# A fused attention and gated feed-forward kernel: VectorE's and ScalarE's side work placed in front of each value block, two kinds of work handed to GpSimd

## The chip, the cores and the metric

The kernel runs on one core of a Trainium2 chip. A core has five engines with an instruction queue each: TensorE (PE, matrix multiplication; PEld are its weight loads), VectorE (DVE), ScalarE (ACT), GpSimd (POOL) and SyncE (SP, which here only issues the DMA transfers). The metric is the device time of one execution in microseconds (us), as the median of several runs. Before the change it is 1805.28 us, the median of three runs from 1804.98 to 1807.15.

## The reference

A token sequence of 2048 rows of 512 is normalized, goes through 32-head softmax attention and, in parallel, through a bilinear gated feed-forward of width 1792, and both are joined:

```python
def _A_ref(x, wqkv, wo):                       # H = 32 heads of Dh = 16
    q, k, v = split(x @ wqkv)
    scores = einsum("bhqd,bhkd->bhqk", q, k) * Dh ** -0.5
    o = einsum("bhqk,bhkd->bhqd", softmax(scores), v)
    return o.transpose(0, 2, 1, 3).reshape(B, S, D) @ wo

def _B_ref(x, w_gate, w_up, w_down):
    h = (x @ w_gate) * (x @ w_up)              # no nonlinearity
    return h @ w_down

xn = layernorm(x)
return x + _A_ref(xn, ...) * silu(_B_ref(xn, ...))
```

Everything is float32. For the projections and the feed-forward the kernel splits each operand into a high part, rounded to a shorter format (F32R), and the low rest, and adds three products: high by high, high by low, low by high.

## The kernel before

**Units, rounds and cycles.** The attention is cut into units: a unit `i` is a group of four heads (`g`, 8 groups) and a block of 512 queries (`c`, 4 blocks), so `NU` = 32 units. A unit has 16 rounds, one for each block of 128 keys; `n` counts all 512 rounds of the main loop (L844 onwards). In a round, for each of the four heads `j`, TensorE makes one transposed score tile of 128 keys by 512 queries (`expo`, L605), of which ScalarE takes the exponential (L607), and one score tile of a later unit (`score`, L580; it runs `LEAD` = 21 rounds ahead), of which VectorE takes the row maximum (L582). Score tiles rotate through three banks (`s`), transposed score tiles and the value blocks' results through three more (`st`), and the fillers below through two (`misc`).

**Value blocks.** After every even round `values()` issues a value block (`block`, L618): TensorE multiplies the exponentials of two earlier rounds (the list `prev`: the two rounds ahead of the current one) with the values and adds them up in a bank. During this block TensorE makes no scores. The block's result is added to the unit's running sum `sums[i]`, a tile named `acc` with one buffer. For a unit's first block ScalarE copies the result into it (L622). For its last block VectorE adds the result (L624). For the six between, ScalarE copies the result out into a tile `e` of the exponentials' ring (L627, `EBUFS` = 12 buffers) and GpSimd adds it (the line of GpSimd's instructions is always L64, that of a helper).

**Finishing a unit.** `finish(i)` is a generator which `step_small(heads)` advances by one `yield` after every round and once in `values()`: VectorE transposes the sum (L636), takes the reciprocals of the softmax denominators (L639), GpSimd multiplies (tile `on`; for the last four units VectorE does, L641), and five rounds later (one round, for the last four units) VectorE transposes back (L645) and a DMA stores the result.

**Fillers.** Between the score tiles TensorE works on a generator of other matrix products: first the remaining query and key projections (`proj_pair`), then the feed-forward (`ffn`: gate `g` and up `u` together, then down `y`), at last the output projection (`ending`, tiles `z`). The class `Filler` spreads each pair of products over whole cycles of two rounds, from an odd round's second head to the next even round's third head. The numbers of filler products in a cycle differ therefore: a gate and up pair takes two or three cycles. When a pair is done, its results have to leave the two `misc` banks: ScalarE copies `g` (L375), VectorE multiplies `h = u * g` (L377), ScalarE rounds `h` to `hh` (L335) and GpSimd takes the rest `hl`; down products are added to `y` (L402; L398 and L400 for the first). GpSimd splits all weights too: `w1h`, `w1l`, `w0h`, `w0l` for gate and up, `dh` and `dl` for down, `fh` and `fl` for the output weights. `silu` goes over the finished `y` in four steps, each a tanh on ScalarE (L341) and two steps on GpSimd.

**What sets the order.** TensorE, ScalarE and VectorE execute in the order of the program text (`manual_schedule`). GpSimd's and SyncE's instructions are ordered by a scheduler. `soon(k, fn)` puts work off by `k` steps, a step being one head of a round (`step()`), so that `fn`'s instructions come behind that head's score tile in each queue. Before the change the product `h` is issued one step after its pair has ended, its rounding four steps after, the second of two additions one step after the first, and a step of `silu` two steps after the third round of four. `flush()` issues everything that still waits.

Of the kernel before, what the change touches and what calls it, by code (L numbers as in the profile page):

```python
# [19 lines left out]
P = 128  # L20
# [29 lines left out]
def body(ctx, tc, x, wqkv, wo, wg, wu, wd, out):  # L50
# [80 lines left out]
    def flush():  # L131
        while waiting:
            waiting.pop(0)[1]()

    def step():
        steps[0] += 1
        while waiting and waiting[0][0] <= steps[0]:
            waiting.pop(0)[1]()


    ep = ctx.enter_context(tc.tile_pool(name="ep", bufs=1))

# [157 lines left out]
    def proj_pair(m, which):  # L300

        outs = []
        yield from pair(outs, [("misc", f"p{w}_{m}_{c}") for _, w, c in which],
                        [terms(lambda d: ws[0][:, d], lambda d: ws[1][:, d],
                               lambda d: xh[c][:, d], lambda d: xl[c][:, d], ND) for ws, _, c in which])
        raws = [qp.tile([P, D], F32, name="qr", bufs=QBUFS) for _ in outs]
        fst["high"] = nc.scalar.activation(raws[0], outs[0], AF.Copy)
        nc.vector.tensor_copy(raws[1], outs[1])
        for o, (_, w, c) in zip(raws, which):
            hl = qp.tile([P, 2, D], F32R, name="hl", bufs=HBUFS)  # L310
            split_rows(o, hl[:, 0], hl[:, 1])
            qk_store(hl, m, w, c)

    def qk_store(hl, m, which, c):

# [15 lines left out]

    later = []

    def hidden(h, hi, lo):
        nc.scalar.activation(hi, h, AF.Copy)  # L335
        pool.tensor_tensor(lo, h, hi, op=OP.subtract)

    def silu(fp, c, y):
        for t in range(4):
# [12 lines left out]
    def ffn(nxt):  # L352
        fp = fst["fp"]
        for c in range(NC):
# [7 lines left out]
            for ti, fs in enumerate(THIRDS):  # L362
# [4 lines left out]
                for i, f in enumerate(fs):  # L367
                    ws = nxt
                    if not (c == NC - 1 and f == NF - 1):
                        nxt = gu_weights((f + 1) % NF)  # L370
                    outs = []
                    yield from pair(outs, [("misc", f"{n}{c}_{f}") for n in "gu"], [terms(lambda d: wh[:, d], lambda d: wl[:, d],
                                                 lambda d: fh[:, d], lambda d: fl[:, d], ND) for wh, wl in ws])
                    g = fp.tile([P, 512], F32, name="g", bufs=1)
                    nc.scalar.activation(g, outs[0], AF.Copy)  # L375
                    h = fp.tile([P, 512], F32, name="h", bufs=1)
                    soon(1, lambda h=h, u=outs[1], g=g: nc.vector.tensor_tensor(h, u, g, op=OP.mult))  # L377
                    soon(4, lambda h=h, hi=hh[:, i], lo=hl[:, i]: hidden(h, hi, lo))
                    raw = fp.tile([P, D], F32, name="wdr", bufs=2)
                    dma(raw, wd[f * P:(f + 1) * P])  # L380
                    pool.tensor_copy(dh[:, i], raw)
                    pool.tensor_tensor(dl[:, i], raw, dh[:, i], op=OP.subtract)
# [7 lines left out]
                for t in range(0, 4, 2):  # L390
                    outs = []
                    yield from pair(outs, [("misc", f"y{c}_{ti}_{u}") for u in (t, t + 1)], [terms(lambda i: hh[:, i, u * P:(u + 1) * P],
                                                 lambda i: hl[:, i, u * P:(u + 1) * P],
                                                 lambda i: dh[:, i], lambda i: dl[:, i], len(fs)) for u in (t, t + 1)])
                    for n, o in enumerate(outs):
                        def add(o=o, y=y[:, t + n], first=ti == 0, n=n):
                            if first and n:
                                nc.vector.tensor_copy(y, o)  # L398
                            elif first:
                                nc.scalar.activation(y, o, AF.Copy)  # L400
                            else:
                                nc.vector.tensor_tensor(y, o, y, op=OP.add)  # L402
                        soon(n if ti else 0, add)
            later.append(silu(fp, c, y))


# [203 lines left out]
    def block(todo):  # L610
# [9 lines left out]
        if todo[0][1] == 0:  # L620
            sums[i] = keep.tile([P, 512], F32, name="acc", bufs=1)
            nc.scalar.activation(sums[i], o, AF.Copy)  # L622
        elif kt >= NT - 2:
            nc.vector.tensor_tensor(sums[i], o, sums[i], op=OP.add)  # L624
        else:
            part = etile()
# [3 lines left out]
    def finish(i):  # L630
# [3 lines left out]
        tn = tr.rearrange("p b e -> p (b e)")  # L634
        yield
        nc.vector.transpose(tn, sums.pop(i))  # L636
        yield
        rc = keep.tile([P, 16, 1], F32, name="rc", bufs=1)
        nc.vector.reciprocal(rc, tr[:, :, DH:DH + 1])  # L639
        late = i >= NU - NC  # L640
        (nc.vector if late else pool).tensor_tensor(on[:, :, 0:DH], tr[:, :, 0:DH], rc.to_broadcast([P, 16, DH]),  # L641
                                                         op=OP.mult)
        for _ in range(1 if late else 5):
            yield
        nc.vector.transpose(tn, on.rearrange("p b e -> p (b e)"))  # L645
        if i == NU - 1:
            fst["tn"] = tn
# [114 lines left out]
    def filler(wq0):  # L762
        yield from proj_pair(0, [(wq0, 0, 2), (wq0, 0, 3)])
        for m in range(1, NG // 2):
            wk, wq = fst.get(("qk", m)) or (qk_weights(m, 1), qk_weights(m, 0))
            for c in range(NC):
# [5 lines left out]
                        tc.add_manual_dep(put.ins, after, BEHIND, reason="not before the first exponentials")  # L772
                if m == NG // 2 - 1 and c == NC - 2:
                    nxt = gu_weights(0)
        flush()
        qkv.close()
        fst["fp"] = ffp.enter_context(tc.tile_pool(name="ffn", bufs=1, reuse_waits="tile"))
# [53 lines left out]
    prev = []  # L831

    def values():
        block(prev)
        if prev[-1][1] == NT - 1:
            heads.append(finish(prev[0][0]))
# [3 lines left out]
    with tc.manual_schedule(engines=ORDERED):  # L840
# [3 lines left out]
        for n in range(NU * 16):  # L844
# [20 lines left out]
                    fil.part(n % 2 and j == 1)  # L865
            if sr == 15 and si < NU:
                maxima(si, 8 if si < NU - 1 else 4)
            step_small(heads)
            if kt % 4 == 2:
                soon(2, lambda: step_small(later))  # L870
            if n == 0:
                run(fst["v"])
            elif n % 2 == 0 or n == NU * 16 - 1:
                values()
            prev.append((i, kt, es))
        block(prev)
        run(finish(NU - 1))
        flush()
# [23 lines left out]
```

## Time and profile before

| | us |
|---|---|
| median of three runs | 1805.28 |
| the profiled execution's own time | 1807.26 |
| its span, from the first to the last instruction | 1805.0 |
| busy: TensorE | 1767.9 |
| busy: VectorE | 1455.0 |
| busy: ScalarE | 1323.7 |
| busy: GpSimd | 821.8 |

The granted TensorE clock was 0.993 of full speed over the span. The times below come from one execution taken by the hardware profiler. A group's row names the line of the kernel, the engine, the operation, the tiles out<-in, their shapes and the count, then the busy time and the mean duration in ns, and at last the idle time of the engine just ahead of the group and what ended it. Where a tile or line is asked for by itself, a row gives shortest, median and longest duration in ns. In an order of time a row begins with its start and its duration in us, and merges consecutive instructions of one kind; brackets hold the idle time ahead and what ended it. A row of the busy time by stretch gives the stretch, its length, and for TensorE, weight loads, VectorE, ScalarE and GpSimd the busy time with the number of instructions, then the granted clock, the transfers' share and GB/s. A matmul's end is modelled, so a busy TensorE is not one at its peak.

### The profile page before, as it was taken

Reading aid. Unit: us, or ns where it says so; the run is one execution under the profiler, and the core shown is the slowest. Engines: PE = TensorE matmul, PEld = TensorE weight load, DVE = VectorE, ACT = ScalarE, POOL = GpSimd, SP = SyncE. Lnnn points to the kernel's source line nnn. Section 1 sums busy time; section 2 is a strip of 40 time slices with the busy share of each in tenths; the row PEclk is TensorE's granted clock in tenths of the full one; section 3 lists DMA queues with packets and bytes.
Section 4 is the critical chain, followed back from the end, with each engine's and each line's share of the span. In section 5 each row is a group of like instructions: output and inputs, shape, how many; then the busy total and the mean of one; then the engine's idle time right before and its main releaser. Section 6 shows DMA issues by size and latency. Waiting matters only on the chain.

```text
span 1805.0 us, 35056 instructions
## 1 busy us (share of the span) xinstructions
PE 1767.9 (98%) x13578; PEld 1056.4 (59%) x13578; DVE 1455.0 (81%) x2471; ACT 1323.7 (73%) x2601; POOL 821.8 (46%) x833
## 2 busy tenths in 40 slices
PE   9999999899999999999999999999999999999997
PEld 6666556556565555555555565665555555555544
DVE  6778888788888888888888888888888888888823
ACT  6357777677777777777777787777778777777673
POOL 5314444643534546344343653534545354345641
PEclk9999999999999999999999999999999999999999
DMA  5316523511231222311024220411224111111431
GB/s 198 115 57 205 217 103 124 145 40 34 69 75 51 75 65 69 75 51 51 28 73 102 80 63 23 103 40 51 85 55 103 40 51 51 35 56 49 143 110 70
DMA packets 117234, 145.78 MB, mean 81 GB/s; under 512 B 12620, under 2 KB 74060, under 8 KB 114380
## 3 DMA queue, kind: packets, MB, share of 16 engines
q1 hardware_dynamic: 117068, 143.55, 27.6%
q8 instruction: 106, 1.74, 0.4%
q14 instruction: 60, 0.49, 0.1%
HBM read 95.94 MB, written 47.45 MB: 79 GB/s over the span
## 4 chain that ended last, share of the span: by engine, by line
PE 86%; DVE 4%; POOL 3%; ACT 2%; DMA 2%; issue 1%; SPq 0%; POOLq 0%; DVEq 0%; ACTq 0%
PE pv L618 25%; PE t L605 17%; PE s L580 12%; PE g L270 5%; PE u L270 4%; PE y L270 4%; PE y L274 4%; PE u L274 3%; PE g L274 3%; DVE mx L582 3%; PE p L270 3%; PE v L251 2%; PE z L270 1%; ACT e L607 1%; PE p L274 1%
## 5 line engine op out<-in xcount | busy, mean ns | idle before, releaser
L582 DVE TENSOR_REDUCE mx<-s 128x1 f32<-128x512 f32 x2048 | 1276.8, 681 | 247.3 <-PE s L580 163.2
L607 ACT ACTIVATE e<-t 128x512 f32<-128x512 f32 x2048 | 1110.8, 609 | 126.4 <-PE t L605 32.2
L605 PE MATMUL t<-qs,ks 50*128 50x512 f32 x2048 | 805.8, 415 | 15.8 <-ACT e L607 14.3
L580 PE MATMUL s<-ks,qs 48*128 48x512 f32 x2048 | 805.0, 423 | 6.1 <-DVE mx L582 5.8
L605 PEld LDWEIGHTS t<-qs,ks 50*128 50x128 f32 x2048 | 360.0, 185 | 327.6 <-issue 162.6
L618 PE MATMUL pv<-e,V 128*32 128x512 f32 x4096 | 495.4, 601 | 0.0
L64 POOL TENSOR_TENSOR acc<-acc,e 128x512 f32<-128x512 f32 x192 | 251.0, 1307 | 455.8 <-ACT e L627 455.8
L580 PEld LDWEIGHTS s<-ks,qs 48*128 48x128 f32 x2048 | 350.7, 185 | 51.9 <-DVE mx L582 23.4
L627 ACT ACTIVATE e<-pv 128x512 f32<-128x512 f32 x192 | 114.7, 598 | 221.6 <-PE pv L618 221.6
L618 PEld LDWEIGHTS pv<-e,V 128*32 128x32 f32 x4096 | 107.4, 109 | 237.0 <-issue 182.7
L64 POOL CAST w0h<-w0r 128x512 fp32r<-128x512 f32 x60 | 36.7, 611 | 154.9 <-PE g L274 68.8
L274 PE MATMUL g<-fh,w1h 64*128 64x512 f32 x224 | 90.7, 405 | 0.0
L274 PE MATMUL y<-dh,hh 64*128 64x512 f32 x224 | 89.7, 401 | 0.0
L270 PE MATMUL y<-dh,hl 64*128 64x512 f32 x224 | 87.9, 392 | 1.7 <-POOL hl L64 1.7
L270 PE MATMUL u<-fh,w0h 64*128 64x512 f32 x224 | 89.1, 398 | 0.0
L274 PE MATMUL u<-fh,w0h 64*128 64x512 f32 x224 | 88.8, 396 | 0.0
L274 PE MATMUL u<-fh,w0l 64*128 64x512 f32 x224 | 88.5, 395 | 0.0
L270 PE MATMUL g<-fh,w1l 64*128 64x512 f32 x224 | 88.4, 395 | 0.0
L270 PE MATMUL g<-fl,w1h 64*128 64x512 f32 x224 | 88.3, 394 | 0.0
L270 PE MATMUL g<-fh,w1h 64*128 64x512 f32 x224 | 88.2, 394 | 0.0
L270 PE MATMUL y<-dh,hh 64*128 64x512 f32 x224 | 88.2, 394 | 0.0
L274 PE MATMUL u<-fl,w0h 64*128 64x512 f32 x224 | 88.1, 393 | 0.0
(257 smaller groups left out, 3065.7 us busy)
## 6 DMA issues: line engine op xcount, KB each, us to landing
w1r<-in_wg_dram SPq DMA_DIRECT2D x56, 256.0 KB
w0r<-in_wu_dram SPq DMA_DIRECT2D x56, 256.0 KB
wdr<-in_wd_dram SPq DMA_DIRECT2D x56, 256.0 KB
qs<-QD SPq DMA_DIRECT2D x64, 192.0 KB
ks<-KD SPq DMA_DIRECT2D x12, 768.0 KB
KD<-hl SPq DMA_DIRECT2D x16, 512.0 KB
QD<-hl SPq DMA_DIRECT2D x16, 512.0 KB
OD<-tr SPq DMA_DIRECT2D x31, 256.0 KB
```

Of the source, the lines that this page charges most:

```text
L64: got = getattr(self.engine, name)(*args, **kw)
L251: nc.tensor.matmul(o, l(d), r(d), start=k == d == 0, stop=k == 2 and d == ND - 1)
L270: nc.tensor.matmul(outs[k], l[LOWER], r[LOWER], start=k == 0 and n == 0, stop=(stop or k == 0) and n == len(low) - 1, skip_group_check=k == 1)
L274: nc.tensor.matmul(outs[1 - k], l[UPPER], r[UPPER], start=k == 0 and m == 0, stop=(stop or k == 0) and m == len(high) - 1, skip_group_chec ...
L580: nc.tensor.matmul(o, QS[i][b:b + KB, pr, t * P:(t + 1) * P], k[b:b + KB, pr, kc * 512:(kc + 1) * 512], start=True, stop=True)
L582: nc.vector.tensor_reduce(MX[i][:, j, t, kc:kc + 1], o, axis=AX.X, op=OP.max)
L605: nc.tensor.matmul(o, k[b:b + KR, pr, kt * P:(kt + 1) * P], QS[i][b:b + KR, pr], start=True, stop=True)
L607: nc.scalar.activation(e, o, AF.Exp, scale=DH ** -0.5)
L618: nc.tensor.matmul(o[32 * j:32 * j + 32], V[:, kt, h0:h0 + 32], es[j], start=n == 0, stop=n == len(todo) - 1)
L627: nc.scalar.activation(part, o, AF.Copy)
```

## The change

A list `before_values` collects work, and `run_ahead()` issues all of it. `values()` calls `run_ahead()` and then advances `finish` by one step, both directly in front of the value block; `step_small(heads)` after every round is gone, so a unit's finish goes on once a cycle, besides the one step when it is put on the list. `finish` has fewer `yield`s: the first transposition and the reciprocal stand together in front of one block, the second transposition in front of the next. On the list go: the product `h` and its rounding; the additions to `y`, both together; of a projection pair, the copy of the second result by VectorE with the splitting and storing behind it. A step of `silu` follows the round at once, which is in front of a block too. TensorE's order of instructions stays as it is.

Two things change engines. `hidden`, which rounded `h` on ScalarE, is replaced by `product`, which multiplies on VectorE and leaves the rounding and the rest to GpSimd (`split_rows`). And the last block's addition to the running sum is done on VectorE only for the last two blocks of the last unit; for the other 31 units ScalarE copies it out and GpSimd adds it, as for the blocks between.

```diff
+    before_values = []
+
+    def run_ahead():
+        while before_values:
+            before_values.pop(0)()
...
         fst["high"] = nc.scalar.activation(raws[0], outs[0], AF.Copy)
-        nc.vector.tensor_copy(raws[1], outs[1])
-        for o, (_, w, c) in zip(raws, which):
-            hl = qp.tile([P, 2, D], F32R, name="hl", bufs=HBUFS)
-            split_rows(o, hl[:, 0], hl[:, 1])
-            qk_store(hl, m, w, c)
+
+        def rest():
+            nc.vector.tensor_copy(raws[1], outs[1])
+            for o, (_, w, c) in zip(raws, which):
+                hl = qp.tile([P, 2, D], F32R, name="hl", bufs=HBUFS)
+                split_rows(o, hl[:, 0], hl[:, 1])
+                qk_store(hl, m, w, c)
+        before_values.append(rest)
...
-    def hidden(h, hi, lo):
-        nc.scalar.activation(hi, h, AF.Copy)
-        pool.tensor_tensor(lo, h, hi, op=OP.subtract)
+    def product(h, u, g, hi, lo):
+        nc.vector.tensor_tensor(h, u, g, op=OP.mult)
+        split_rows(h, hi, lo)
...
-                    soon(1, lambda h=h, u=outs[1], g=g: nc.vector.tensor_tensor(h, u, g, op=OP.mult))
-                    soon(4, lambda h=h, hi=hh[:, i], lo=hl[:, i]: hidden(h, hi, lo))
+                    before_values.append(lambda h=h, u=outs[1], g=g, hi=hh[:, i], lo=hl[:, i]: product(h, u, g, hi, lo))
...
-                        soon(n if ti else 0, add)
+                        before_values.append(add)
...
-        elif kt >= NT - 2:
+        elif i == NU - 1 and kt >= NT - 2:
             nc.vector.tensor_tensor(sums[i], o, sums[i], op=OP.add)
...
         nc.vector.transpose(tn, sums.pop(i))
-        yield
         rc = keep.tile([P, 16, 1], F32, name="rc", bufs=1)
...
-        for _ in range(1 if late else 5):
-            yield
+        yield
         nc.vector.transpose(tn, on.rearrange("p b e -> p (b e)"))
...
+        run_ahead()
         flush()
         qkv.close()
...
     def values():
+        run_ahead()
+        step_small(heads)
         block(prev)
...
-            step_small(heads)
             if kt % 4 == 2:
-                soon(2, lambda: step_small(later))
+                step_small(later)
...
+        run_ahead()
         block(prev)
         run(finish(NU - 1))
         flush()
```

## The prediction

> **What bounds the kernel now.** I read the page first, then the busy time by stretch, then VectorE's instructions in order of time.
>
> ```profile
> span 1805.0 us, 35056 instructions
> PE 1767.9 (98%) x13578; PEld 1056.4 (59%) x13578; DVE 1455.0 (81%) x2471; ACT 1323.7 (73%) x2601; POOL 821.8 (46%) x833
> PE 86%; DVE 4%; POOL 3%; ACT 2%; DMA 2%; issue 1%; SPq 0%; POOLq 0%; DVEq 0%; ACTq 0%
> ```
>
> TensorE looks full, but its busy time can't be taken at its word. I call a cycle the two rounds from the start of one value block (L618) to the next; there are 256. These are six cycles and one with a tanh, cut from block start to block start:
>
> ```profile
> 807.85:814.43 6.58, 6.34 (x53) 3.71 (x56) 5.17 (x10) 5.25 (x11) 2.75 (x4) 1.00 0.05 16
> 840.17:846.98 6.81, 6.58 (x54) 3.77 (x53) 5.82 (x10) 4.99 (x11) 1.45 (x3) 1.00 0.02 3
> 664.44:671.17 6.73, 6.36 (x51) 3.12 (x51) 5.76 (x11) 5.37 (x12) 5.75 (x7) 1.00 0.34 86
> 1094.35:1100.32 5.97, 5.97 (x48) 3.30 (x52) 4.81 (x9) 4.74 (x11) 1.30 (x1) 1.00 0.20 62
> 1100.32:1107.14 6.82, 6.82 (x61) 4.35 (x64) 6.67 (x13) 4.98 (x10) 0.00 (x0) 1.00 0.03 7
> 1177.85:1183.83 5.98, 5.98 (x53) 3.72 (x52) 4.88 (x9) 4.40 (x10) 2.09 (x3) 1.00 0.09 34
> 1183.83:1190.54 6.71, 6.71 (x61) 4.19 (x60) 6.45 (x13) 5.72 (x13) 5.60 (x6) 1.00 0.27 78
> ```
>
> The first number is the length, the second TensorE's busy time with its instructions in brackets. Full cycles (61 matmuls) take 6.71 us, light ones (48 to 53) only 5.98, and 48 matmuls seem to fill TensorE as well as 61. So light cycles are not bound by TensorE. VectorE's order of time says by what:
>
> ```profile
> 810.21 2.48 DVE L582 TENSOR_REDUCE mx<-s 128x1 f32<-128x512 f32 x4 [1.41 <-PE t L605]
> 812.61 0.70 DVE L645 STREAM_TRANSPOSE tr<-on 128x512 f32<-128x512 f32 x1
> ...
> 836.34 4.87 DVE L582 TENSOR_REDUCE mx<-s 128x1 f32<-128x512 f32 x8 [1.21 <-PE s L580]
> 842.20 0.69 DVE L624 TENSOR_TENSOR acc<-pv,acc 128x512 f32<-128x512 f32 x1 [0.99 <-PE pv L618]
> ...
> 845.20 0.70 DVE L636 STREAM_TRANSPOSE tr<-acc 128x512 f32<-128x512 f32 x1
> 845.83 2.44 DVE L582 TENSOR_REDUCE mx<-s 128x1 f32<-128x512 f32 x4
> 848.19 0.67 DVE L377 TENSOR_TENSOR h<-u,g 128x512 f32<-128x512 f32 x1
> 848.79 0.23 DVE L639 RECIPROCAL rc<-tr 128x16 f32<-128x16 f32 x1
> 849.37 5.15 DVE L582 TENSOR_REDUCE mx<-s 128x1 f32<-128x512 f32 x8 [0.35 <-PE s L580]
> ```
>
> Eight maxima cost 4.87. Between two runs of eight VectorE idles 1.2 to 1.4 us, while TensorE is in the value block and makes no scores. In a light cycle scores wait for maxima: 4.87 plus the hole is the 5.98. The hole can be filled: the block of 846.98 meets the product at 848.19, 1.21 later; product and reciprocal go into the hole and the next maximum starts at 849.37, 2.39 after the block's start. So **2.39 - 1.21 = 1.18 us of VectorE work right ahead of a block costs nothing**. Work in the middle of a run does cost: the second transposition (812.61) makes a light cycle 6.58 instead of 5.98; the last sum (842.20) with the first transposition (845.20) makes one 6.81. In a full cycle that pair costs 6.82 - 6.71, mostly hidden behind TensorE.
>
> **The gains.** Prices of the parts:
>
> ```profile
> L624 DVE TENSOR_TENSOR acc<-pv,acc 128x512 f32<-128x512 f32 x33 | 22.8, 691 | 30.3 <-PE pv L618 28.7 <-POOL w0l L64 0.8
> L335 ACT ACTIVATE hh<-h 128x512 fp32r<-128x512 f32 x56 | 36.4, 651 | 0.0
> L341 ACT ACTIVATE e<-y 128x512 f32<-128x512 f32 x16 | 10.3, 645 | 0.0
> L64 POOL CAST dh<-wdr 128x512 fp32r<-128x512 f32 x56 | 33.6, 612 | 62.1 <-PE y L274 32.0 <-DMA wdr<-in_wd_dram 22.6 <-PE y L270 7.1
> L64 POOL TENSOR_TENSOR acc<-acc,e x192: 1253/1307/1337, 125.1 to 1779.6; 128x512 f32<-128x512 f32 x192
> L636 DVE STREAM_TRANSPOSE tr<-acc x32: 698/699/712, 162.4 to 1783.7; 128x512 f32<-128x512 f32 x32
> L645 DVE STREAM_TRANSPOSE tr<-on x32: 698/700/712, 181.7 to 1785.2; 128x512 f32<-128x512 f32 x32
> ```
>
> (a) Last sums leave VectorE for all units but the last, and the first transposition moves ahead of the next block with the reciprocal: 0.70 + 0.23 = 0.93, under 1.18, so free. The eighth cycle of a unit becomes an ordinary one. Of 30 such cycles before the tail, 14 are light (0.60 to 0.84 over an ordinary one, 0.73 on average: 10.2 us), 2 between (0.34), 14 full (0.09 each): **12.1 us**. (b) The second transposition goes ahead of the block after that, 0.70, free: 18 light third cycles lose 0.37 to 0.61: **9.0 us**; the full ones gain nothing. (c) The tanh stands in mid-run now and delays exponentials: 664.44:671.17 is a light cycle of 6.73 where such a cycle without it takes 6.21 by the trace's other block starts. Ahead of a block ScalarE has a hole too (1.23 us in the ACT rows below). Six light cycles: **2.8 us**. (d) The rounding of h leaves ScalarE (0.65 each, 56 times), nearly always hidden now: **0.5 us**. Together 24.4. The product h stands behind the same maximum as before: nothing. The additions to y move by one maximum: nothing.
>
> **The costs on VectorE.** The unit's running sum has one buffer, so ScalarE's first copy of the next unit can't start before the first transposition has read the old one. It starts 1.96 after the block (row 666.40); the transposition ends 1.21 + 0.70 = 1.91. That fits by 0.05. Where a product or a projection's copy stands ahead of it (9 units in the new order), it ends 0.6 later, the copy too, and with it the score bank that TensorE wants back: 0.55 each, **5.0**. Two units have two additions to y ahead: 1.2 late, 0.2 of it lost already, **1.8**. Two light cycles with additions and the maxima's reduction overrun the hole by 0.3: **0.6**.
>
> **The costs on GpSimd.** It gets 31 sums of 1.307 and 56 castings of 0.612, 74.8 us more. What matters is when a running sum is done: the part it reads lies in the exponentials' ring, and the eighth exponential behind it takes the buffer over. What lateness does is here already:
>
> ```profile
> 666.40 0.60 ACT L627 ACTIVATE e<-pv 128x512 f32<-128x512 f32 x1 [1.23 <-PE pv L618]
> 667.85 0.65 ACT L341 ACTIVATE e<-y 128x512 f32<-128x512 f32 x1
> ...
> 256.60 0.60 ACT L607 ACTIVATE e<-t 128x512 f32<-128x512 f32 x1 [1.89 <-POOL acc L64]
> 257.09 0.59 ACT L627 ACTIVATE e<-pv 128x512 f32<-128x512 f32 x1
> ```
>
> ```profile
> ACT e L607 <- POOL acc L64: 22.4, 9, 6.8
> ```
>
> Nine exponentials wait so, 22.4 us in all. An eighth exponential has about 1.2 us to spare, since ScalarE waits for the block anyhow; beyond this the part's copy is late and the cycle longer. A cycle with a product, on GpSimd, with its block at 827.90:
>
> ```profile
> 827.49 0.61 POOL L64 CAST w0h<-w0r 128x512 fp32r<-128x512 f32 x1 [2.36 <-PE u L270]
> 829.85 1.31 POOL L64 TENSOR_TENSOR w1l<-w1r,w1h 128x512 fp32r<-128x512 f32 x1
> 831.10 1.32 POOL L64 TENSOR_TENSOR acc<-acc,e 128x512 f32<-128x512 f32 x1
> 832.47 1.28 POOL L64 TENSOR_TENSOR hl<-h,hh 128x512 fp32r<-128x512 f32 x1
> ```
>
> In the new order casting and rest of h stand ahead of that sum: it starts at 831.1 + 0.6 + 1.3 = 833.0 and ends at 834.3, 6.4 after the block. Even in a light cycle 7.5 would do: its length 6.0, the eighth exponential 0.3 after the next block's start, 1.2 to spare. So the castings cost nothing in an ordinary cycle. Where a chain of down weights and a tanh's two steps come ahead too, it is late:
>
> ```profile
> 1347.03 1.27 POOL L64 TENSOR_TENSOR acc<-acc,e 128x512 f32<-128x512 f32 x1
> 1348.27 0.61 POOL L64 TENSOR_SCALAR e<-e 128x512 f32<-128x512 f32 x1
> 1348.97 1.28 POOL L64 TENSOR_TENSOR y<-e,y 128x512 f32<-128x512 f32 x1
> ```
>
> The new order puts those two (1.9) ahead of this sum, which is late as it is: 2.9; a like place near 670 us 1.1; the output weights near 1650 us pass 1.8 on; a projection's end at the fourth unit 0.9; one more 0.2: **6.9**. In the tail the last sum of unit 30 goes behind eight GpSimd steps that end with this one:
>
> ```profile
> 1738.83 1.28 POOL L64 TENSOR_TENSOR dh<-e,hl 128x512 fp32r<-128x512 f32 x1
> ...
> 1739.88 0.60 ACT L622 ACTIVATE acc<-pv 128x512 f32<-128x512 f32 x1 [1.24 <-PE pv L618]
> ```
>
> It ends near 1742.8 with another sum put ahead, the transposition 0.7 later, so ScalarE's first copy of unit 31 starts at 1743.5 instead of 1739.9: 3.6, and 0.6 from outputs queued before it: **4.2**. Bounds of all GpSimd terms: 0 if waits for transfers swallow them, 20 if each of some 28 cycles with both a product and another step pays 0.7. I take 11.1, by the rows at these places.
>
> [...]
>
> **Sum.** 24.4 - (5.0 + 1.8 + 0.6 + 6.9 + 4.2) = 5.9. The profiled execution took 1807.26 (span 1805.0 and 2.3 around it), so 1801.4; the runs' median, 1805.28, is 2.0 lower than that execution: **1799.4**.
>
> **Rivals.** (B) GpSimd is in time: of the costs only 5 remain, 1805.3 - 19 = 1786. For it: its idle time, and the chains above wait for transfers. Against: nine waits of the exponentials for its sums today. (C) *Slower*: GpSimd late in ordinary cycles. One mechanism: every product cycle's sum behind the casting. It decides once such a sum ends 1.1 later than the 6.4 above, past the 7.5; with a loss of 0.25 on average over 56 cycles it is +14, so 1799.4 + 14 = 1813. For it: each of these chains grows by 1.9. Against: the 1.1. (D) The 0.05 of spare ahead of ScalarE's first copy is not there: 20 more units lose 0.3, +6, so 1805: the gain is given back one cycle later. (E) GpSimd's added 74.8 us hold VectorE up in light cycles, half of all: +37, 1836. [...]
>
> **How the numbers follow.** The forecast has 0.52 (alone 1794 to 1804), B 0.17, C 0.17, D 0.12, E 0.02. About 0.2%, 3.6 us, is what a measurement of this kernel can tell from no change. Of the forecast 0.37 lies below 1801.7, the rest within; with B that makes faster 0.54; D is half within, half beyond, C nearly all beyond: same 0.24, slower 0.22. Range 1786 to 1813.
>
> **What would show it.** Right: light eighth cycles at 6.0 to 6.2 instead of 6.81, light third cycles at 6.0 instead of 6.58, VectorE's transpositions at 1.2 after a block, its instructions 31 fewer. Costs: nine first copies (now 1.96 after the block) at 2.6; waits of the exponentials for GpSimd's sums above today's. Wrong: these waits gone (B), in most product cycles (C), first copies late in nearly all units (D), transpositions over 0.71 us (E).

## The result, and the profile after

Over 14 runs each, the changed kernel took 1802.65 us (1797.37 to 1805.76) and the kernel before 1807.14 us (1802.41 to 1809.21): a ratio of **0.9977, 95% interval 0.9967 to 0.9987**, some 4 us faster. The prediction had 1799.4 us and 5.9 us faster. The profiled execution of the changed kernel took 1804.02 us against 1807.26 before.

The page of the changed kernel, its span, the engines' busy time and the chain that ended last:

```profile
span 1802.2 us, 35104 instructions
PE 1758.0 (98%) x13578; PEld 1064.8 (59%) x13578; DVE 1447.8 (80%) x2440; ACT 1326.7 (74%) x2576; POOL 891.8 (49%) x920
PE 86%; POOL 6%; DMA 2%; issue 2%; DVE 2%; ACT 2%; SPq 0%; POOLq 0%; ACTq 0%; DVEq 0%
```

VectorE has 31 instructions fewer and GpSimd is busy for 70.0 us more, where the prediction had worked out 74.8. GpSimd's share of the chain doubled, from 3% to 6%. The instructions of TensorE stand in the same order in both kernels, so every cycle (block start to block start; I number the 256 from 0 at the first block) can be compared with its own counterpart. Five of the cycles that the prediction showed, in the stretch view of the changed kernel (length, then busy time and instructions of TensorE, its weight loads, VectorE, ScalarE and GpSimd):

```profile
799.48:805.47 5.99, 5.99 (x50) 3.72 (x48) 4.59 (x8) 4.66 (x11) 2.08 (x3) 1.00 0.01 3
831.18:837.16 5.98, 5.98 (x50) 3.73 (x48) 4.65 (x8) 4.64 (x11) 2.05 (x3) 1.00 0.03 5
658.43:664.64 6.21, 6.21 (x48) 3.33 (x46) 5.41 (x12) 5.38 (x12) 5.24 (x7) 1.00 0.26 87
1081.48:1087.46 5.98, 5.98 (x46) 3.32 (x44) 4.83 (x9) 4.75 (x10) 1.30 (x1) 1.00 0.20 61
1087.46:1094.16 6.70, 6.70 (x57) 4.21 (x56) 6.20 (x11) 5.53 (x11) 1.31 (x1) 1.00 0.03 7
```

In this order: the light third cycle (6.58 before), the light eighth (6.81), the light one with a tanh (6.73), an ordinary light one (5.97) and a full eighth (6.82). VectorE has eight instructions left in the first two, the maxima alone. The work that was in mid-run is in the hole, and where a product stands ahead of it too (VectorE, then ScalarE, in order of time) it looks so:

```profile
833.61 4.88 DVE L589 TENSOR_REDUCE mx<-s 128x1 f32<-128x512 f32 x8 [1.33 <-PE s L587]
838.41 0.68 DVE L343 TENSOR_TENSOR h<-u,g 128x512 f32<-128x512 f32 x1
839.00 0.70 DVE L643 STREAM_TRANSPOSE tr<-acc 128x512 f32<-128x512 f32 x1
839.74 0.25 DVE L645 RECIPROCAL rc<-tr 128x16 f32<-128x16 f32 x1
839.91 2.50 DVE L589 TENSOR_REDUCE mx<-s 128x1 f32<-128x512 f32 x4
...
839.80 0.60 ACT L629 ACTIVATE acc<-pv 128x512 f32<-128x512 f32 x1 [1.54 <-PE t L612]
```

The block starts at 837.16. Product, transposition and reciprocal end at 839.99, 2.83 after it, and ScalarE's first copy starts 2.64 after it, as the prediction said for such units (2.6 instead of 1.96).

Summed over its cycles, changed kernel minus before, the change had gained 16.5 us when cycle 235 was done (near 1637 us), and the last 20 cycles gave some 13 of them back. So the question of this case is where the time went. The waits of the changed kernel (idle time, times, longest):

```profile
ACT e L614 <- POOL acc L64: 52.9, 36, 6.7
DVE tr L643 <- POOL acc L64: 8.1, 2, 7.3
ACT acc L629 <- DVE tr L643: 9.2, 9, 2.1
```

The exponentials' waits for GpSimd's sums, 22.4 us and 9 times before, are 52.9 and 36 times. Four places hold most of the loss: cycles 189 (9.94 us, 6.35 before), 235 and 236 (20.6, 16.2), 243 and 244 (21.9, 15.1) and 248 (11.7, 5.9).

The longest of them, in the stretch view of the changed kernel; the column behind the engines is the granted clock of TensorE:

```profile
1637.00:1640.00 3.00, 2.67 (x22) 0.60 (x18) 1.75 (x5) 0.38 (x1) 1.20 (x2) 1.00 0.38 131
1640.00:1644.00 4.00, 0.00 (x0) 0.00 (x0) 0.44 (x1) 0.00 (x0) 3.74 (x5) 0.92 0.22 66
1644.00:1647.00 3.00, 2.30 (x10) 2.17 (x12) 0.77 (x2) 2.19 (x5) 1.50 (x3) 0.50 0.01 2
1647.00:1651.00 4.00, 4.00 (x26) 3.43 (x26) 3.11 (x5) 2.73 (x5) 0.00 (x0) 0.60 0.00 0
```

```profile
1638.72 0.61 POOL L64 CAST w0h<-wdr 128x512 fp32r<-128x512 f32 x1 [2.31 <-DMA wdr<-OD]
1639.41 1.26 POOL L64 TENSOR_TENSOR w0l<-wdr,w0h 128x512 fp32r<-128x512 f32 x1
1640.85 0.61 POOL L64 CAST w0h<-wdr 128x512 fp32r<-128x512 f32 x1 [0.18 <-DMA wdr<-OD]
1641.54 1.26 POOL L64 TENSOR_TENSOR w0l<-wdr,w0h 128x512 fp32r<-128x512 f32 x1
1642.76 1.26 POOL L64 TENSOR_TENSOR acc<-acc,e 128x512 f32<-128x512 f32 x1
...
1644.05 0.60 ACT L614 ACTIVATE e<-t 128x512 f32<-128x512 f32 x1 [6.68 <-POOL acc L64]
```

GpSimd stands with the sum behind two transfers and what it does with them; the eighth exponential waits 6.68 us for its buffer; TensorE has nothing at all for 4 us, and then runs at half of its clock, for 6.8 us by the trace's record of the clock (0.50 from 1643.35 to 1650.18). The wait costs once by itself and once more by the clock behind it.

### The profile page after: what moved, and what is told of

It is laid out like the page before. It is cut to its first block, busy times and chain, and to the rows that moved or that the text cites. A ratio compares the mean times of both kernels' runs of the same rounds, so it can differ in the third digit from the quotient of the medians.

```text
span 1802.2 us, 35104 instructions
## 1 busy us (share of the span) xinstructions
PE 1758.0 (98%) x13578; PEld 1064.8 (59%) x13578; DVE 1447.8 (80%) x2440; ACT 1326.7 (74%) x2576; POOL 891.8 (49%) x920
## 3 DMA queue, kind: packets, MB, share of 16 engines
q8 instruction: 106, 1.74, 0.4%
## 4 chain that ended last, share of the span: by engine, by line
PE 86%; POOL 6%; DMA 2%; issue 2%; DVE 2%; ACT 2%; SPq 0%; POOLq 0%; ACTq 0%; DVEq 0%
PE pv L625 23%; PE t L612 17%; PE s L587 12%; PE g L275 5%; PE y L275 5%; PE g L279 4%; PE u L275 4%; PE y L279 4%; PE u L279 3%; PE p L275 2%; PE v L256 2%; PE p L279 1%; PE z L275 1%; POOL acc L64 1%; DVE mx L589 1%
## 5 line engine op out<-in xcount | busy, mean ns | idle before, releaser
L614 ACT ACTIVATE e<-t 128x512 f32<-128x512 f32 x2048 | 1117.7, 605 | 125.5 <-POOL acc L64 52.9
L612 PEld LDWEIGHTS t<-qs,ks 50*128 50x128 f32 x2048 | 363.7, 187 | 330.3 <-ACT e L614 131.1
L64 POOL TENSOR_TENSOR acc<-acc,e 128x512 f32<-128x512 f32 x223 | 290.8, 1304 | 484.3 <-ACT e L634 481.7
L634 ACT ACTIVATE e<-pv 128x512 f32<-128x512 f32 x223 | 133.3, 598 | 229.8 <-PE pv L625 229.6
L275 PE MATMUL y<-dl,hh 64*128 64x512 f32 x224 | 88.6, 396 | 0.0
L275 PE MATMUL u<-fl,w0h 64*128 64x512 f32 x224 | 88.4, 395 | 0.0
L279 PE MATMUL u<-fl,w0h 64*128 64x512 f32 x224 | 88.4, 395 | 0.0
```

The lines of the kernel that those rows point to most:

```text
L64: got = getattr(self.engine, name)(*args, **kw)
L275: nc.tensor.matmul(outs[k], l[LOWER], r[LOWER], start=k == 0 and n == 0, stop=(stop or k == 0) and n == len(low) - 1, skip_group_check=k == 1)
L279: nc.tensor.matmul(outs[1 - k], l[UPPER], r[UPPER], start=k == 0 and m == 0, stop=(stop or k == 0) and m == len(high) - 1, skip_group_chec ...
L612: nc.tensor.matmul(o, k[b:b + KR, pr, kt * P:(kt + 1) * P], QS[i][b:b + KR, pr], start=True, stop=True)
L614: nc.scalar.activation(e, o, AF.Exp, scale=DH ** -0.5)
L634: nc.scalar.activation(part, o, AF.Copy)
```

## The experiments

Each kernel below ran in five rounds beside the kernel before, on one chip for each group of four, and each ratio is to the runs of the kernel before in its own group. Cycles are read in one profiled execution each.

**First group.** Both moves between engines undone and only the places left (the rounding stands four steps, which is one round, behind the product, not four rounds as the expectation says):

```diff
-    def product(h, u, g, hi, lo):
-        nc.vector.tensor_tensor(h, u, g, op=OP.mult)
-        split_rows(h, hi, lo)
+    def hidden(h, hi, lo):
+        nc.scalar.activation(hi, h, AF.Copy)
+        pool.tensor_tensor(lo, h, hi, op=OP.subtract)
...
-        elif i == NU - 1 and kt >= NT - 2:
+        elif kt >= NT - 2:
```

> The changed kernel with both moves between engines undone (last sums back on VectorE, rounding of h back on ScalarE, four rounds after the product); only the new places ahead of the value blocks are left. My theory: the gains come from the places and the extra stalls from GpSimd's 75 us of added work. Then this keeps the third cycles (about -9 us) and the tanh cycles (-2.5), about half of the eighth cycles' 12 (the last sum, 0.70 us, is again in mid-run there), and loses the stalls near 1330, 1637, 1700 and 1731 us of the span (3.6, 5.1, 6.7 and 5.8 us): 0.990 to 0.994 of before, 10 us or so faster than the changed kernel (0.9977). The exponentials' waits for GpSimd's sums, 52.9 us in the changed kernel, fall to 15 to 25 us (22.4 before). Rival: the stalls come from the new places themselves (work ahead of the block delays ScalarE's copies, or the tanh's GpSimd steps come sooner): then they stay, and the time is 0.998 to 1.002 of before.

Measured: 1797.65 us, ratio **0.9949** (0.9937 to 0.9961), some 5 us faster than the changed kernel, though just outside the 0.990 to 0.994 that was expected. Cycles 236 (7.6 us) and 248 (5.9) are free of their stalls, 189 (10.0) and 243 and 244 (21.9) are not. The waits of its exponentials:

```profile
ACT e L615 <- POOL acc L64: 32.3, 13, 6.2
```

They fell, but not to the 25 or less that was expected. So half of the theory holds: two of the stalls come from the moves between engines, the other two from the places, as the rival had it.

The complement, the kernel before with the two moves between engines only (its last sums as in the changed kernel, the rounding by `split_rows` at its old place):

```diff
-        nc.scalar.activation(hi, h, AF.Copy)
-        pool.tensor_tensor(lo, h, hi, op=OP.subtract)
+        split_rows(h, hi, lo)
...
-        elif kt >= NT - 2:
+        elif i == NU - 1 and kt >= NT - 2:
```

> The kernel before with only the two moves between engines (last sums and the rounding of h on GpSimd), everything at its old place. Theory: the moves don't pay by themselves. The first transposition stands some 3.5 us behind the last block of a unit, and GpSimd's last sum ends later than that, so VectorE waits for it 1 to 2.5 us in most of 31 units, in the light ones with TensorE behind it: 1.005 to 1.02 of before, with VectorE's waits for GpSimd's sums at 30 us or more (8.1 in the changed kernel). Rival: GpSimd is early enough, and taking 0.70 us out of each eighth cycle is a gain by itself: 0.995 to 0.999.

Measured: 1828.88 us, ratio **1.0124** (1.0110 to 1.0137). VectorE's transpositions wait for GpSimd's last sums:

```profile
DVE tr L635 <- POOL acc L64: 27.9, 14, 6.0
```

That is half of the units, not most, but longer each time. The eighth cycles as a whole lose 17.2 us where the changed kernel gains 12.2. Cycles 236 (13.7) and 248 (11.3) stall here too, 189 (6.0) and 243 and 244 (15.1) do not: the exact complement of the run before.

The thirteenth buffer, for the changed kernel and, as a control, for the kernel before:

```diff
-EBUFS = 12
-HBUFS = 2
+EBUFS = 13
+HBUFS = 1
```

> The changed kernel with 13 buffers in the exponentials' ring instead of 12 (the room comes from the projections' stored halves, one buffer instead of two, which can only cost in the first 440 us of the span). Theory: the end's losses are the eighth exponential waiting for GpSimd's sum of the part whose buffer it takes over. With a thirteenth buffer it takes that one, so the exponentials' waits for GpSimd's sums fall from 52.9 to under 15 us, the long cycles near 1330, 1637, 1700 and 1731 us shrink to under 9 us, and the time is 0.986 to 0.992 of before. Rival: GpSimd is late anyway (it waits for transfers, and the next wait, of the part's copy or the transposition, takes over): the waits change their name and the time stays within 0.2% of the changed kernel's 0.9977.

> The kernel before with the same thirteenth buffer and single stored half. Theory: before has fewer such waits (22.4 us, 9 times), so it gains less than the changed kernel does from the same buffer: 0.994 to 0.999 of before. Rival: the buffer helps both alike (as much as in the changed kernel, 6 us or more on either), and then it says nothing on GpSimd's added work.

Measured: 1823.70 us, ratio 1.0091 (1.0079 to 1.0104), and 1829.71 us, 1.0125 (1.0112 to 1.0139). Both expectations fail, since the room was not free: with the single stored half the first 48 cycles of the two are 15 and 17 us longer than those of the kernel before. Behind these the changed kernel is 2.9 us faster with the buffer than without, the kernel before 1.8 us slower. The wait has changed its name (the copy of the part, not the exponential, now waits for GpSimd's sum):

```profile
ACT e L634 <- POOL acc L64: 51.9, 14, 7.7
```

With 51.9 us of such waits the stalls at 236 (13.4), 243 and 244 (21.2) and 248 (10.7) stay; 189 falls to 7.5. So one buffer more doesn't take the other stalls away.

**Second group.** One edit at a time in the changed kernel. The tanh's two GpSimd steps put later in the program:

```diff
-            pool.tensor_scalar(e, e, 0.5, 0.5, op0=OP.mult, op1=OP.add)
...
+            def rest(t=t, e=e):
+                pool.tensor_scalar(e, e, 0.5, 0.5, op0=OP.mult, op1=OP.add)
...
+            soon(2, rest)
```

> The changed kernel with the tanh still ahead of the value block on ScalarE, but its two GpSimd steps (1.9 us) two score rounds' steps later, behind the part's sum. Theory: the stalls that stayed with the new places alone (cycle 189 at 10.0 us, 85 at 7.0, 243 and 244 at 8.6 and 13.3) come from these two steps standing ahead of a sum, not from the tanh itself. Then 189 and 85 fall back to 6.0 to 6.5 us, 243 and 244 together from 21.9 to 15 to 17, the tanh cycles keep their 0.5 each, and the time is 0.992 to 0.995 of before (the changed kernel: 0.9977). Cycles 236 (13.6) and 248 (11.7) stay. Rival: GpSimd's queue is too long there whatever the order; then these cycles stay within 1 us of what they are, and the ratio within 0.001 of 0.9977.

Measured: 1802.57 us, ratio 0.9975 (0.9966 to 0.9985). This says nothing on the theory, since GpSimd's instructions came out in the same order as in the changed kernel: the planner orders GpSimd by itself and put the steps ahead of the sum again. It serves as a second measurement of the changed kernel (0.9977).

The last sums of units 28 to 30 back on VectorE:

```diff
-        elif i == NU - 1 and kt >= NT - 2:
+        elif i >= NU - NC and kt >= NT - 2:
```

> The changed kernel with the last sums of the last four units (not only of the very last) on VectorE. Theory: cycle 248 (11.7 us, 5.9 before the change) is unit 30's last sum behind eight GpSimd steps; it falls under 7 us, the rest stays: 0.994 to 0.9955 of before. Rival: GpSimd's backlog at that place holds an exponential anyway, as it did without the change; then 248 stays over 10 us and the ratio near 0.9977.

Measured: 1800.01 us, ratio 0.9964 (0.9952 to 0.9977). Cycle 248 is back at 5.87 us. First the changed kernel (from 1730.75), then this one:

```profile
1730.75:1736.00 5.25, 2.47 (x21) 0.71 (x19) 0.72 (x2) 0.88 (x3) 4.46 (x5) 0.95 0.38 138
1736.00:1742.48 6.48, 6.48 (x28) 4.71 (x28) 1.38 (x3) 4.51 (x8) 0.00 (x0) 0.51 0.23 74
```

```profile
1732.02:1737.89 5.87, 5.87 (x49) 3.42 (x45) 0.45 (x1) 4.61 (x11) 3.25 (x4) 1.00 0.55 169
```

The cycle went as expected, 5.9 us shorter; the two ratios are 0.0013 apart, 2.4 us, less than expected, and their intervals overlap.

The rounding of h back on ScalarE (the first part of the diff at the top):

> The changed kernel with h rounded on ScalarE again, four score steps behind the block, and only the rest on GpSimd. Theory: cycle 236 (13.6 us, 8.5 before; 7.6 with both moves undone, 13.7 with both moves alone) comes from the rounding's 0.6 us ahead of GpSimd's output weights, so it falls under 9 us, while 189, 243 and 244 and 248 stay: 0.9945 to 0.996 of before. Rival: it is the last sums that move GpSimd's queue there; then 236 stays over 12 us and the ratio is 0.997 to 0.999.

Measured: 1802.67 us (1796.31 to 1804.15), ratio 0.9975 (0.9965 to 0.9985). In the profiled execution, the fastest of its ten, cycle 236 is free of the stall and 235 has 2.2 us of it:

```profile
1626.97:1636.23 9.26, 7.52 (x54) 4.24 (x50) 5.52 (x10) 4.83 (x10) 7.89 (x9) 0.82 0.31 88
1636.23:1643.00 6.77, 6.14 (x56) 4.09 (x52) 4.99 (x10) 4.89 (x10) 3.30 (x4) 1.00 0.11 37
```

So the rounding is what makes GpSimd late there (one execution, but four more kernels with the new places and the rounding on ScalarE agree, as told below), while in the median nothing is gained by this edit alone: the ratio is that of the rival.

Every last sum back on VectorE, directly behind its block (`elif kt >= NT - 2`):

> The changed kernel with every unit's last sum on VectorE again, directly behind its block, and the rounding still on GpSimd. Theory: cycle 248 falls under 7 us (-5), and the eighth cycles lose about 3 of the 12 us they gained (the changed kernel gains 3 us more in cycles 48 to 234 than the places alone, and this is where); 236 stays over 12 us: 0.996 to 0.998 of before. Rival: 236 goes with the sums (under 9 us), then 0.993 to 0.995.

Measured: 1802.25 us, ratio 0.9978 (0.9968 to 0.9988). 248 is free (5.9 us), the eighth cycles gain 8.7 instead of 12.2, and 236 stays at 13.2: theory, not rival.

**Third group.** The tanh's steps behind the part's sum again, now by an order on GpSimd that the planner can't change:

```diff
+            fst["sum"] = pool.tensor_tensor(sums[i], sums[i], part, op=OP.add).ins.name
...
+                half = pool.tensor_scalar(e, e, 0.5, 0.5, op0=OP.mult, op1=OP.add)
+                tc.add_manual_dep(half.ins, fst["sum"], ORDER, reason="behind the part's sum")
```

> The changed kernel with the tanh ahead of the value block, and its two GpSimd steps tied behind the part's sum by an order on GpSimd (in e8_steps_behind the planner, which orders GpSimd by itself, had left them where they were). Theory: at 189 GpSimd waits for a down weight, then does it (1.9 us), the tanh's steps (1.9) and only then the sum; with the sum 1.9 earlier TensorE's gap of 2.34 us there falls under 1 us, and with it the stretch of half clock behind it: 189 at 6.0 to 7.0 us (9.9), 85 at 6.0 to 6.4 (7.0), 243 and 244 together at 15 to 18.5 (21.9); 236 and 248 stay: 0.993 to 0.996 of before. Rival: the down weight's transfer alone makes the sum late; then 189 stays over 9 and the ratio within 0.001 of 0.9977.

Measured: 1799.43 us, ratio 0.9963 (0.9951 to 0.9975), just outside what was expected. 189 is 6.95 us and 85 is 5.98, as expected; 243 is 6.7, but 244 is longer (14.2), and the pair, 20.9, misses the 15 to 18.5. At 189, GpSimd in the changed kernel and then in this one:

```profile
1329.07 0.61 POOL L64 CAST dh<-wdr 128x512 fp32r<-128x512 f32 x1 [2.15 <-DMA wdr<-in_wd_dram]
1329.76 1.28 POOL L64 TENSOR_TENSOR dl<-wdr,dh 128x512 fp32r<-128x512 f32 x1
1331.01 0.62 POOL L64 TENSOR_SCALAR e<-e 128x512 f32<-128x512 f32 x1
...
1331.78 1.27 POOL L64 TENSOR_TENSOR y<-e,y 128x512 f32<-128x512 f32 x1
1333.01 1.26 POOL L64 TENSOR_TENSOR acc<-acc,e 128x512 f32<-128x512 f32 x1
```

```profile
1329.37 0.61 POOL L64 CAST dh<-wdr 128x512 fp32r<-128x512 f32 x1 [2.43 <-DMA wdr<-in_wd_dram]
1330.06 1.28 POOL L64 TENSOR_TENSOR dl<-wdr,dh 128x512 fp32r<-128x512 f32 x1
...
1331.48 1.27 POOL L64 TENSOR_TENSOR acc<-acc,e 128x512 f32<-128x512 f32 x1
```

Counted from the block's start (1330.24 and 1329.82), the weight comes 0.7 us later than in the changed kernel, and the sum still starts 1.1 us earlier. The cycle is 3.0 us shorter, more than the 1.1, since the clock isn't halved behind it any more; first the changed kernel, then this one:

```profile
1334.00:1336.00 2.00, 1.05 (x10) 0.91 (x12) 0.48 (x1) 1.70 (x4) 0.74 (x2) 1.00 0.36 121
1336.00:1340.00 4.00, 4.00 (x24) 3.32 (x20) 3.10 (x6) 2.81 (x6) 1.29 (x2) 0.57 0.01 4
```

```profile
1329.82:1336.77 6.95, 6.10 (x52) 3.49 (x50) 5.13 (x10) 4.42 (x9) 6.16 (x8) 1.00 0.24 79
```

Combinations: the new places with the rounding on ScalarE and GpSimd's last sums for the first 28 units only; the new places alone with the tied order; and the first with the tied order.

> The new places, the last sums on GpSimd only for the first 28 units, and the rounding of h on ScalarE. Theory: the two stalls that single edits took away (236 by the rounding, 248 by the late sums) go together, 189 and 243 and 244 stay: 0.994 to 0.996 of before; against the new places alone (0.9949) the sums of the first 28 units on GpSimd are worth 3 us in the eighth cycles, so it is at least as fast as these. Rival: what remains at 189 and at 243 and 244 varies between executions by as much as the two gave; then it is 0.996 to 0.998.

> The new places alone (0.9949), with the tanh's GpSimd steps tied behind the part's sum. Theory: the stalls left there (189 at 10.0, 243 and 244 at 21.9 together) go as in e9_sum_first, 189 to 6.0 to 7.0 and the pair to 15 to 18.5: 0.991 to 0.9935 of before, the fastest so far. Rival: they stay, and it is 0.9945 to 0.9955.

> e10 with the tanh's GpSimd steps tied behind the part's sum. Theory: all four stalls are gone and the eighth cycles keep their full gain: 0.989 to 0.9925 of before, 2 to 4 us faster than e11. Rival: GpSimd's added sums are not needed once the places are right; then it equals e11 within 0.001.

Measured: 1795.13 us, ratio 0.9942 (0.9930 to 0.9955); 1794.35 us, 0.9935 (0.9921 to 0.9949); and 1790.53 us (1788.17 to 1793.24), **0.9917 (0.9903 to 0.9932)**, the fastest of all, 15 us ahead of the kernel before. The last one's page and its cycles 189, 236, 244 and 248:

```profile
span 1787.1 us, 35079 instructions
PE 1751.5 (98%) x13578; PEld 1054.4 (59%) x13578; DVE 1447.8 (81%) x2443; ACT 1337.7 (75%) x2629; POOL 857.4 (48%) x861
```

```profile
1330.54:1337.00 6.46, 6.10 (x50) 3.58 (x48) 5.04 (x10) 4.42 (x10) 5.78 (x7) 1.00 0.26 85
1633.97:1642.40 8.43, 6.13 (x50) 4.07 (x48) 5.09 (x10) 4.48 (x10) 5.14 (x6) 1.00 0.11 35
1690.44:1704.44 14.00, 7.71 (x50) 5.42 (x48) 1.52 (x5) 5.37 (x12) 11.28 (x12) 0.76 0.54 172
1723.00:1728.89 5.89, 5.89 (x47) 3.59 (x45) 1.05 (x2) 4.65 (x11) 3.32 (x4) 1.00 0.58 186
```

In the second of the three the ratio is at the edge of what was expected, but the pair of 243 and 244 stays at 21.6. In the third, three of the four stalls are gone (the theory had all four). The fourth, near 1700 us, stands in every kernel with the new places, and no run removed it. The 3.8 us between the last two kernels' medians agree with the 3 us that the last sums on GpSimd are worth in the eighth cycles, though their intervals overlap.

## Why the prediction was right, and where its sizes were off

**The gains** came much as worked out. The eighth cycles give 12.2 us (12.1 predicted), the third ones 10.5, of them 1.3 in one early cycle that was not meant (9.0 predicted), the tanh cycles 0.5 each in five (2.8 predicted in six). Which part of (a) does it was not told apart in the prediction: with the last sums left on VectorE the eighth cycles still give 8.7, so the place of the transposition carries most of it and the move to GpSimd 3.5. The engines alone, at the old places, cost 22 us. Taking the rounding off ScalarE, set at 0.5, is worth 1.6 in cycles 48 to 234 against the kernel with it back on ScalarE, when 189 and 232, which are longer with it, are left out.

**The costs on VectorE** were 4.4 instead of 7.4. Nine first copies stood behind a product or a projection's copy, as forecast. Four of them began 2.62 or 2.63 us after the block, all in full cycles, and these cycles are 0.5 longer; the other five began 2.14 after it, and their cycles are no longer than before. So the 0.55 was charged to nine units where four pay it. One of the four, cycle 232, lost 0.9 more, in another way (told under the rivals); that makes 2.8. The two units with two additions cost 0.5 each (0.9 predicted), the two light cycles 0.3 each, as predicted. Rival D has fallen: it wanted ScalarE's first copy late in 20 units more, and that copy waits for the transposition 9 times in all.

**The costs on GpSimd** are the term that was mis-sized: 11.1 predicted, 20.6 measured, just above the upper bound of 20 that stood in the text. Most places were the right ones: 0.98 at the fourth unit (0.9 predicted), 1.0 near 670 us (1.1), 3.6 near 1330 (2.9). Too small were the output weights near 1640 (4.4 for 1.8), and the outputs of the tail, put at 0.6: cycles 242 to 244 cost 5.4. Two cycles that were not named (35 and 195) cost 1.7. The last sum of unit 30 (3.6 predicted) costs 5.8 in its own cycle, and 3.7 over cycles 247 to 250, for the next ones run faster. Smaller gains all over the other cycles, 2.9 in sum, made up for part of it.

So the forecast's way of adding up was right, but it is luck in part that the total came near. The gains that were named came to 25.3 us and the costs to 25.0; the 3.2 us between the two profiled executions are what the smaller gains left. The 9.5 us by which GpSimd's costs were too small were made up by 3.0 on VectorE, 1.4 in the named gains and 2.4 in gains that were not counted.

What the sum had left out is the clock behind a wait. I priced a late sum at the time by which it is late. The exponential at 1644.05 waits 6.68, against some 1.2 that a cycle has to spare, so 5.5. But cycle 236 is 6.8 longer than where the stall is gone (6.77, with the rounding back on ScalarE); the 1.3 between the two are, by my estimate, TensorE's half clock behind the wait. The clock falls near 1336 and 1736 us too. In the rows above it is 0.50 behind 1644 us, 0.57 behind 1336 and 0.51 behind 1736; in the kernel before, cycle 236 has the full clock (1.00):

```profile
1653.45:1661.94 8.49, 6.15 (x54) 4.08 (x53) 5.12 (x11) 4.49 (x10) 5.24 (x6) 1.00 0.12 34
```

Rivals: (B), GpSimd in time, fell with the 52.9 us of waits. (C) asked for lateness in ordinary product cycles; these show next to none, the loss is in four places. (E) fell as a cost in half of all cycles: the transpositions take 702 ns in the median, where they took 699 and 700, with 70 us more on GpSimd beside them.

```profile
L643 DVE STREAM_TRANSPOSE tr<-acc x32: 699/702/712, 164.9 to 1780.8; 128x512 f32<-128x512 f32 x32
L650 DVE STREAM_TRANSPOSE tr<-on x32: 698/702/714, 171.7 to 1782.3; 128x512 f32<-128x512 f32 x32
```

But VectorE held up beside GpSimd, as (E) has it, is in the trace, in an instruction that the prediction did not look at: in cycle 232 VectorE's multiplication `on` takes 1.38 us while GpSimd takes the rest of `h`, and 0.42 where the rounding is back on ScalarE and GpSimd idle beside it (0.42 also at 1736.28 in the changed kernel, where GpSimd is idle). First the changed kernel, then that one:

```profile
1612.07 1.28 POOL L64 TENSOR_TENSOR hl<-h,hh 128x512 fp32r<-128x512 f32 x1
1612.25 1.38 DVE L647 TENSOR_TENSOR on<-tr,rc 128x256 f32<-128x256 f32 x1
```

```profile
1609.28 0.42 DVE L648 TENSOR_TENSOR on<-tr,rc 128x256 f32<-128x256 f32 x1
```

Cycle 232 is 8.1 us in the six profiles with the new places and the rounding on GpSimd, and 7.2 in the five with the new places and the rounding on ScalarE. The kernel before shows the same at 1736.85, where `on` takes 0.87 beside GpSimd. VectorE does this multiplication for the last four units only, so the price is small here. What makes it longer there, no run shows.

**What causes the stalls**, by the runs:

- Near 1330 it is the tanh's two steps ahead of a sum behind a late transfer. The tied order shows it: cycle 189 takes 6.4 to 7.0 us in the three profiles with it and 7.1 to 10.2 in the eight others with the new places. The 7.1 is from an execution in which the weight came 1.4 us earlier by the blocks, so the late transfer is needed too.
- Near 1640 it is the rounding of h ahead of the output weights: cycle 236 takes 12.9 to 13.8 us in the seven profiles with it on GpSimd and 6.8 to 10.2 in the six experiments without it; 235 and 236 together take 19.9 to 20.8 and 16.0 to 17.9. A part of the lateness is in the kernel before as well: the two take 16.2 us in it where two full ones take 13.4.
- Near 1731 it is the last sum of unit 30: cycle 248 takes 10.6 to 12.3 us in the six profiles with it on GpSimd and 5.9 in the eight others.
- Near 1700 it is one of the places, since it is there without the moves between engines and not there with these alone; the tied order moved it from one cycle to the next. The traces narrow it further. Unit 29's second transposition, which now stands a block behind the first, comes 1.84 us into cycle 241 instead of 4.82 us into cycle 240. Its result is stored and loaded again (`wdr` from `OD`) for the output projection. This load is issued 5.5 us later, and GpSimd waits for it 6.9 to 8.6 us in the eleven profiles with the new places, 2.6 to 2.8 us in the three with the old ones. What GpSimd does behind this transfer comes later with it, among it ten output steps that stand ahead of a sum. So the prediction's "free" for the second transposition probably does not hold for a unit whose output is needed at once. No run moved it back by itself, so this stays open.

That undoing either move between engines alone gave nothing in the median (0.9975 and 0.9978), and undoing both 5 us, is only partly understood: each move's gain (3.5 and 1.6 us) is lost with its stall. By the cycles of the profiled executions, undoing the sums should have gained some 1.6 us and undoing the rounding some 4; each ratio's interval reaches 1.8 us to either side, and the other stalls differ in size between the profiled executions (243 and 244 take 20.9 to 23.7 us with the new places). The changed kernel's 14 runs spread over 8.4 us, the five of the places alone over 1.9.

## What to carry to other kernels

Work of a second engine could here be had for nothing in the stretch where it waited for TensorE anyway: look for the idle time between its runs and put the small jobs there, up to what fits, here 1.18 us. Moving work to an engine with half of its time idle was not free here (GpSimd, busy for 46%; 20.6 us of costs), where sums stood in its queue behind waits for transfers: look at what stands ahead of the one result that others wait for, at the worst place and not on average. Look also at every kind of instruction that will run beside the moved work: here VectorE's multiplication `on` took three times as long beside GpSimd (1.38 us instead of 0.42), while its maxima took 684 ns on average instead of 681 and its transpositions 702 instead of 699 and 700. And price a gap in TensorE's work with the slower clock behind it (here 0.50 behind the gap that ends near 1644 us), not with its length alone.

## What the runs showed of the hardware that was not expected

The granted clock of TensorE was 0.50 for one or two stretches of 3.41 us (once three) behind many gaps in its work, and within a trace these stretches begin whole multiples of 3.413 us apart: between 400 and 1800 us at 1336.15, 1643.35, 1708.20, 1735.51, 1752.58 and 1786.71 in the changed kernel, which is 90, 19, 8, 5 and 10 of them, and at 1748.73, 1755.56 and 1789.69 in the kernel before, 2 and 10. I call this the grid. Over the 14 profiled executions (the kernel before, the changed one and the twelve of the experiments), behind the first 320 us, the gaps between the end of one matmul and the start of the next (ends are modelled) stand so to the granted clock just behind them:

| gap | cases | half clock behind it | one stretch | two stretches |
|---|---|---|---|---|
| 1.0 to 1.5 us | 11 | 1 | 1 | 0 |
| 1.5 to 1.7 us | 4 | 0 | 0 | 0 |
| 1.7 to 2.6 us | 26 | 14 | 13 | 1 |
| 2.6 to 4.0 us | 25 | 25 | 14 | 11 |
| over 4.0 us | 30 | 30 | 3 | 26 |

In the kernel before and the changed one alone, the gaps without half clock behind them were 1.12, 1.74, 1.96, 2.34 and 2.51 us long, those with it 2.34, 2.78, 3.48 (twice), 4.10, 4.34, 5.03 and 5.64.

The gap's length alone did not tell in which case the clock fell. Over the same executions, the stretches of the grid with the full clock can be sorted by the share for which TensorE was busy. All 57 with under 45% were followed by half clock, 13 of 24 with 45 to 55%, 1 of 13 with 55 to 65%, and of 5820 with more only 23, all of them 60 to 50 us before the end (in the kernel before and the changed one alone: 7 of 7, 1 of 6, 0 of 2 and 3 of 833). In these 23 the modelled ends leave no gap over 0.36 us, but TensorE starts only 6 to 11 matmuls, where 20 to 32 are common; what lowers the clock there stays open.

So it was about even whether the clock fell behind a gap of 1.7 to 2.6 us (14 of 26). One of 2.34 us was followed by it near 1332 us in the changed kernel, where nearly all of it lies in one stretch of the grid (35% busy), and not near 1656 us in the kernel before, where it lies across two (77 and 55% busy). First the changed kernel in stretches of the grid, then the kernel before; the granted clock stands behind the five engines:

```profile
1332.74:1336.15 3.41, 1.20 (x10) 1.06 (x12) 1.26 (x2) 1.85 (x4) 2.15 (x3) 1.00 0.36 126
1336.15:1339.56 3.41, 3.41 (x18) 2.93 (x18) 2.62 (x5) 2.43 (x5) 0.70 (x2) 0.50 0.02 5
```

```profile
1653.15:1656.57 3.42, 2.63 (x22) 0.61 (x18) 2.25 (x6) 0.33 (x1) 3.18 (x4) 1.00 0.20 52
1656.57:1659.98 3.41, 1.86 (x16) 1.86 (x18) 1.21 (x2) 2.51 (x5) 2.33 (x3) 1.00 0.13 49
1659.98:1663.40 3.42, 3.42 (x34) 2.03 (x30) 3.42 (x7) 2.69 (x6) 0.03 (x1) 1.00 0.00 0
```

A gap of 4.34 us was followed by one stretch in one kernel and by two in three others. A kernel with gaps near this size may so lose a stretch in one run and not in the next, which is the likely reason for the spread of the runs; that was not tried by itself.

Of the 51 gaps of 1.7 to 4.0 us, 39 were followed by the half clock, so gaps of this size have to be planned for in a kernel like this one.
